# An attention scan fused with a router: matmuls regrouped by array shape, one-hot rows moved to another engine, and table work moved in the order

## The chip, the cores and the metric

The kernel runs on one core of a Trainium2 chip. The metric is device microseconds (us) of one execution. A core has five engines that work side by side, each through its own list of instructions in order: PE (TensorE, matrix products), DVE (VectorE), ACT (ScalarE), POOL (GpSimd) and SP (SyncE, which issues DMA transfers). Engines wait for each other through semaphores.

## The reference

The program chains three layers; the output of one is the input of the next.

```python
def _attn_ref(q, k, v, alpha):            # 4 batches, 8 heads, 768 steps, head size 48
    state = np.zeros((B, H, D, D))
    for t in range(S):
        state = alpha[:, :, t, :, None] * state + np.einsum('bhd,bhe->bhde', k[:, :, t], v[:, :, t])
        y[:, :, t] = np.einsum('bhd,bhde->bhe', q[:, :, t], state)

def _moe_ref(x, w_gate, w_noise, noise, w1, w2):   # 3072 tokens of 384, 8 experts of 1024
    noisy_logits = x @ w_gate + np.log1p(np.exp(x @ w_noise)) * noise
    # the two largest per token; softmax over the two (+ 1e-9 in the denominator)
    for e in range(E):
        for k in range(2):
            mask = top2[:, k] == e
            out[mask] += top2_w[mask, k, None] * (np.maximum(x[mask] @ w1[e], 0.0) @ w2[e])

def _moe2_ref(x, w_gate, w_val, w_out):            # 384 -> 1536 -> 384
    gate = 1.0 / (1.0 + np.exp(-(x @ w_gate)))
    return (gate * (x @ w_val)) @ w_out
```

Inputs are float32, but for the three weights of the last layer, which are float64 and are turned into float32 on the chip.

## The kernel before

**Attention and router.** The scan is done in 6 chunks of 128 steps by 4 pairs of heads: 24 units u = (chunk c, pair p), batches side by side. The order of every engine is written out by hand in this stage. `unit` issues, in turn: the scores of unit u+1 (`st_S`, tile `sc`, L110; copied by ACT to `am` and masked on POOL by an affine_select, L113), the steps of the router's slot TURN, the output (`st_Y`, tile `y`: state part L136, masked part L141), the new state (`st_U`, tile `uu`: the old state through an identity matrix, L154, and keys by values, L159), transposes (`st_K`, L121; `st_R`, L177), the slot COUNT, the scaled copy of the state on ACT, the products of decays three units ahead on DVE (`st_T`, L92 to L98), and the slots DECIDE and LAST. So an instruction that stands late in a unit on PE or DVE keeps the next unit's work behind it.

A chunk's router steps are spread over the units that follow by a table `when`, one pair (unit after the chunk's end, slot) per step: logits (L188), softplus and noise (`router_soft`), choice of two experts (`router_choice`, L331 to L347, with 0/1 rows `mb`), counting by triangular and all-ones matrices (`router_count`, L359 to L362), rank within the expert (`router_rank`, L375 to L395), then the table of rows: for k = 0, 1 a one-hot of the low seven bits of the rank times the token number (`ohl`, eight ACT operations, L410 and L413), a one-hot of the expert and the high bits (`ohh`, DVE, L416), four matmuls into a tile `tb` (L423) and an add into `tab` on DVE (L426). After chunk 3 the table is cast to indices (L449), and the first half of expert 0 is gathered from DRAM by POOL (`early_fetch`, L532).

**Experts.** Each of 8 experts runs in two halves. Float32 operands are split in a high and a low part, and each product takes three matmuls (L507 to L509). Weights come in pieces of 128x768: SP loads `raw`, ACT copies the high part `whi` (L455), and the low part `wlo` is a subtraction (L456) on POOL; for four pieces of expert 0, amid attention, on DVE (`by_vector`). The router steps of the last two chunks run amid expert 0 (list `late`), then `ready` casts the second table and gathers expert 0's second half. Amid the other experts `narrow` turns float64 weights into float32 by three DVE operations (L499 to L501).

**Last layer.** Blocks of 384 tokens: each token's two result rows are gathered by POOL (`grow`, L828), weighted and added on DVE (L831, L832), transposed on PE (`pt`, L840), and run through gate (`pg`, then `sg`), value and output. From expert 0 on, the order is set by a planner that places recorded instructions engine by engine.

## Time and profile before

| | us |
|---|---|
| three runs | 1130.45, 1137.29, 1139.26 |
| median | 1137.29 |
| profiled execution | 1136.44 |
| its span | 1134.7 |
| PE busy | 1090.0 (96%) |
| DVE, ACT, POOL busy | 469.7, 405.2, 312.0 |

The span is the time between the first and the last recorded instruction. A busy time adds up the instructions of an engine, so an engine that works at half the clock is busy for longer. "PEclk" is the clock that was granted to PE in a stretch, 1.00 for 2.4 GHz and 0.50 for 1.2 GHz. Waits are named by the instruction that ended last before the waiting one could start.

### The profile page before, as it was taken

To read this page: it belongs to the slowest core of one execution; us is meant where nothing else is said; L and a number is where in the kernel's file an instruction comes from. 1 tells how busy PE (TensorE), PEld (TensorE's weight loads), DVE (VectorE), ACT (ScalarE), POOL (GpSimd) and SP (SyncE) were. 2 spreads that over 40 slices of the span, in tenths; PEclk is the share of its full clock that TensorE was granted. 3 is DMA by queue.
4 is the path that set the end of the run, shared out by engine and by line. 5 is a ranking of instruction groups with operands and counts; after the bars stand their busy time and mean duration, and the time that the engine had idled before them with its cause. 6 is when DMAs were issued, how large, how long until landed. Compare 5 with 4: busy or idle time off the path is not lost. (4 is left out here: it accounts for less than half of the span.)

```text
span 1134.7 us, 17977 instructions
## 1 busy us (share of the span) xinstructions
PE 1090.0 (96%) x7202; PEld 1039.6 (92%) x7202; DVE 469.7 (41%) x998; ACT 405.2 (36%) x902; POOL 312.0 (27%) x258
## 2 busy tenths in 40 slices
PE   7999988899999999999999989999999999999998
PEld 7777778799898989999999889999999999999998
DVE  8977766325436353534222343052423232313131
ACT  4676657423233333334233425031313131313131
POOL 3332234623333333434331737220101011000000
PEclk8988889999999999999999999999999999999999
DMA  8655523524545454645332531211010101010000
GB/s 230 195 168 169 165 95 112 164 70 143 198 138 188 151 182 157 212 157 184 92 104 56 165 94 49 65 42 43 17 48 14 49 13 51 9 35 1 22 1 21
DMA packets 48072, 115.45 MB, mean 102 GB/s; under 512 B 6464, under 2 KB 24800, under 8 KB 47984
## 3 DMA queue, kind: packets, MB, share of 16 engines
q1 hardware_dynamic: 41456, 94.60, 26.8%
q0 software_dynamic: 6528, 19.67, 5.7%
q8 instruction: 57, 0.93, 0.3%
q14 instruction: 31, 0.25, 0.1%
HBM read 87.50 MB, written 26.74 MB: 101 GB/s over the span
## 5 line engine op out<-in xcount | busy, mean ns | idle before, releaser
L456 POOL TENSOR_TENSOR wlo<-raw,whi 128x768 fp32r<-128x768 f32 x78 | 144.7, 1863 | 250.4 <-ACT whi L455 246.2
L507 PE MATMUL pg<-x2h,whi 128*128 128x384 f32 x576 | 195.2, 339 | 2.6 <-DVE sg L858 2.6
L509 PE MATMUL pg<-x2h,wlo 128*128 128x384 f32 x576 | 193.3, 336 | 0.0
L508 PE MATMUL pg<-x2l,whi 128*128 128x384 f32 x576 | 193.3, 336 | 0.0
L570 DVE SCALAR_TENSOR_TENSOR h<-ph,h 128x384 fp32r<-128x384 f32 x192 | 78.9, 442 | 202.5 <-ACT h L567 195.5
L858 DVE TENSOR_TENSOR sg<-sg,pg 128x384 f32<-128x384 f32 x96 | 53.1, 553 | 213.8 <-PE pg L509 198.8
L507 PE MATMUL ph<-xh,whi 128*128 128x384 f32 (+1 forms) x384 | 136.3, 356 | 2.2 <-DVE h L570 1.6
L508 PE MATMUL ph<-xl,whi 128*128 128x384 f32 (+1 forms) x384 | 136.1, 354 | 0.0
L509 PE MATMUL ph<-xh,wlo 128*128 128x384 f32 (+1 forms) x384 | 135.7, 353 | 0.0
L507 PE MATMUL py<-whi,h 128*128 128x384 f32 x384 | 132.9, 346 | 0.8 <-ACT yrow L593 0.6
L508 PE MATMUL py<-wlo,h 128*128 128x384 f32 x384 | 127.9, 335 | 0.0
L567 ACT ACTIVATE h<-ph 128x448 fp32r<-128x448 f32 (+1 forms) x128 | 65.4, 516 | 174.8 <-PE ph L509 173.3
L509 PE MATMUL py<-whi,h 128*128 128x384 f32 x384 | 118.4, 337 | 3.6 <-DVE h L570 3.6
L828 POOL DMA_INDIRECT grow<-yd,row x48 | 46.9, 977 | 266.7 <-PE pt L840 198.1
L507 PEld LDWEIGHTS pg<-x2h,whi 128*128 128x128 f32 x576 | 108.7, 189 | 3.1 <-DVE sg L858 2.9
L509 PEld LDWEIGHTS pg<-x2h,wlo 128*128 128x128 f32 x576 | 108.7, 189 | 0.0
L508 PEld LDWEIGHTS pg<-x2l,whi 128*128 128x128 f32 x576 | 108.6, 189 | 0.0
L455 ACT ACTIVATE gh<-sg 128x384 fp32r<-128x384 f32 x96 | 50.3, 524 | 140.7 <-DVE sg L858 136.3
L507 PE MATMUL po<-whi,gh 128*128 128x384 f32 x288 | 96.3, 334 | 2.1 <-issue 2.1
L509 PE MATMUL po<-whi,gl 128*128 128x384 f32 x288 | 96.2, 334 | 0.0
L508 PE MATMUL po<-wlo,gh 128*128 128x384 f32 x288 | 96.2, 334 | 0.0
L455 ACT ACTIVATE whi<-raw 128x768 fp32r<-128x768 f32 x82 | 68.6, 842 | 65.2 <-DMA raw<-in_w2h_dram 43.4
(169 smaller groups left out, 1778.2 us busy)
## 6 DMA issues: line engine op xcount, KB each, us to landing
ur<-in_uh_dram SPq DMA_DIRECT2D x23, 675.5 KB
raw<-in_w1h_dram SPq DMA_DIRECT2D x32, 384.0 KB
raw<-in_w2h_dram SPq DMA_DIRECT2D x32, 384.0 KB
yd<-yrow SPq DMA_DIRECT2D x48, 192.0 KB
w<-t SPq DMA_DIRECT2D x36, 192.0 KB
raw<-w SPq DMA_DIRECT2D x18, 384.0 KB
xv<-in_vh_dram SPq DMA_DIRECT2D x6, 768.0 KB
xd<-xr SPq DMA_DIRECT2D x6, 768.0 KB
```

The source lines that it names most:

```text
L455: a = nc.scalar.activation(hi, src, AF.Copy)
L456: b = e.tensor_tensor(lo, src, hi.bitcast(FT), op=OP.subtract)
L507: nc.tensor.matmul(out, wh, mh, start=first, stop=False)
L508: nc.tensor.matmul(out, wh, ml, start=False, stop=False)
L509: nc.tensor.matmul(out, wl, mh, start=False, stop=last)
L567: a = nc.scalar.activation(h[:, :tot], p[:, :tot], AF.Relu)
L570: b = nc.vector.scalar_tensor_tensor(h[:, lo:lo + j - i], p[:, i:j], 0.0, h[:, i:j].bitcast(FT), op0=OP.max, op1=OP.subtract)
L828: nc.gpsimd.indirect_dma_start(out=r, out_offset=None, in_=src, in_offset=bass.IndirectOffsetOnAxis(ap=g.row[:, n, k:k + 1], axis=0))
L858: nc.vector.tensor_tensor(sg, sg, pp[1], op=OP.mult)
```

## The change

Seven things are done:
- The eight score matmuls of a unit, 48 rows by 128 columns of the array, become sixteen of 64x64 tiles (row group j, column half h); the identity product of the state is split in column pieces of 64 and 48. Groups of equal array shape now follow one another.
- A one-hot row is one POOL operation (compare, then multiply) in place of two ACT operations.
- Tables of chunks 0 to 3 are summed in a PSUM bank (`g.ptab`, the tile `wm`), with one copy at the end in place of eight adds.
- Rank keeps counts in a spare column of `mb`; rows and weights of tokens are computed once for all chunks (`router_rows`) in `ready`, amid expert 0.
- In `when` the first table matmul moves from (3, COUNT) to (4, COUNT) and the second to (5, COUNT), with their one-hots and adds; `early_fetch` moves one unit later.
- `by_vector` goes: the four early lower halves of weights are computed on POOL.
- The first operations of `narrow` and of the weighted rows become scalar_tensor_tensor with a broadcast second input; in the last expert weight steps are issued behind the last gather.

```diff
         for b in range(B):
-            for j in range(2):
-                sl = slice(64 * j, 64 * j + D)
-                nc.tensor.matmul(s[j][:, b], KT[u][sl, b, :], Q[u][sl, b, :], start=True, stop=True)
+            for h in range(2):
+                for j in range(2):
+                    sl, hs = slice(64 * j, 64 * j + D), slice(64 * h, 64 * h + 64)
+                    nc.tensor.matmul(s[j][hs, b], KT[u][sl, b, hs], Q[u][sl, b, :], start=True, stop=True)
         for j in range(2):
             nc.scalar.activation(am[:, j], s[j], AF.Copy)
             g.last_mask = nc.gpsimd.affine_select(out=am[:, j], in_=am[:, j], pattern=[[0, B], [1, C]],
...
         if c:
-            nc.tensor.matmul(o[:RW].rearrange("p b e -> p (b e)"), ident[:RW, :RW], st[p][:RW, :B * D], start=True,
-                             stop=False, skip_group_check=True)
+            for j in range(2):
+                hs = slice(64 * j, min(64 * j + 64, RW))
+                nc.tensor.matmul(o[hs].rearrange("p b e -> p (b e)"), ident[:RW, hs], st[p][:RW, :B * D], start=True,
+                                 stop=False, skip_group_check=True)
         for b in range(B):
             for j in range(2):
                 h0 = b * HD + (2 * p + j) * D
...
-    w = t("w", [128, B, 3])
-    nc.vector.tensor_tensor(w[:, :, 0], m8[:, :, 1], m8[:, :, 0], op=OP.subtract)
-    nc.scalar.activation(w[:, :, 1], w[:, :, 0], AF.Exp)
-    v.update(ei=ei, m=m, mb=mb, w=w)
-
-
-def router_count(tc, g, v):
+    nc.vector.tensor_tensor(m, g.iota8.rearrange("p (k b) e -> p k b e", k=2), ei[:, :, :, None].to_broadcast([128, 2, B, E]),
+                            op=OP.is_equal)
+    nc.vector.tensor_tensor(g.mb[c % 2][:, 0:B], m[:, 0], m[:, 1], op=OP.add)
+    v["m"] = m
+
+
+def router_count(tc, g, c, v):
 
     nc = tc.nc
     B, E = g.B, g.E
...
+    g.run = g.mb[(c + 1) % 2][:, B]
+    with nc.allow_low_precision("counts up to 24 are exact"):
+        nc.vector.tensor_reduce(g.run, g.mb[c % 2].rearrange("p b e -> p e b"), axis=mybir.AxisListType.X, op=OP.add)
     if c > g.c0:
         rs = t("rs", [128, B, E])
         nc.vector.tensor_tensor(rs, rk, g.roff[:, None, :].to_broadcast([128, B, E]), op=OP.add)
         rk = rs
-    for k in range(2):
-        nc.vector.tensor_tensor(m[:, k], m[:, k], rk, op=OP.mult)
-    rank = t("rank", [128, 2, B])
-    nc.vector.tensor_reduce(rank.rearrange("p k b -> p (k b)"), m.rearrange("p k b e -> p (k b) e"), axis=mybir.AxisListType.X, op=OP.add)
+    nc.vector.tensor_tensor(m, m, rk[:, None].to_broadcast([128, 2, B, E]), op=OP.mult)
+    nc.vector.tensor_reduce(rank, m, axis=mybir.AxisListType.X, op=OP.add)
     ri = t("ri", [128, 2, B], I32)
     nc.vector.tensor_copy(ri, rank)
     nc.vector.tensor_scalar(ri, ri, 7, None, op0=OP.logical_shift_right)
     nc.vector.scalar_tensor_tensor(kb(g.code[:, T]), ei, float(g.N // 128), ri, op0=OP.mult, op1=OP.add)
     nc.vector.scalar_tensor_tensor(kb(g.low[:, T]), ri, -128.0, rank, op0=OP.mult, op1=OP.add)
-    nc.vector.tensor_scalar(g.nlow[:, T], g.low[:, T], -1.0, None, op0=OP.mult)
-    nc.vector.tensor_scalar(ei, ei, float(g.cap), None, op0=OP.mult)
-    nc.vector.scalar_tensor_tensor(kb(g.row[:, T]), rank, float(g.cap - 1), ei, op0=OP.min, op1=OP.add)
-    nc.vector.tensor_scalar(w[:, :, 2], w[:, :, 1], 1.0, 1e-9, op0=OP.add, op1=OP.add)
-    nc.vector.reciprocal(g.wts[:, T, 0], w[:, :, 2])
-    nc.vector.tensor_tensor(g.wts[:, T, 1], w[:, :, 1], g.wts[:, T, 0], op=OP.mult)
+
+
+def router_rows(tc, g, rw):
+
+    nc = tc.nc
+    t = lambda name, shape: rw.tile(shape, FT, name=name, tag=name, bufs=1)
+    w = t("w", [128, g.NT, 2])
+    nc.vector.tensor_tensor(w[:, :, 0], g.m8[:, :, 1], g.m8[:, :, 0], op=OP.subtract)
+    nc.scalar.activation(w[:, :, 0], w[:, :, 0], AF.Exp)
+    nc.vector.tensor_scalar(w[:, :, 1], w[:, :, 0], 1.0, 1e-9, op0=OP.add, op1=OP.add)
+    nc.vector.reciprocal(g.wts[:, :, 0], w[:, :, 1])
+    nc.vector.tensor_tensor(g.wts[:, :, 1], w[:, :, 0], g.wts[:, :, 0], op=OP.mult)
+    e = t("ec", [128, g.NT, 2])
+    nc.vector.tensor_scalar(e, g.ei, float(g.cap), None, op0=OP.mult)
+    nc.vector.scalar_tensor_tensor(g.row, g.rank, float(g.cap - 1), e, op0=OP.min, op1=OP.add)
 
 
 def router_table(tc, g, c):
...
-            nc.scalar.activation(lo[:, b], g.iotaP, AF.Abs, bias=g.nlow[:, n, k:k + 1])
-        for b in range(B):
-            n = c * B + b
-            nc.scalar.activation(lo[:, b], lo[:, b].bitcast(FT), AF.Relu, bias=g.ids[:, n:n + 1], scale=g.nids[:, n:n + 1])
+            nc.gpsimd.tensor_scalar(lo[:, b], g.iotaP, g.low[:, n, k:k + 1], g.ids[:, n:n + 1], op0=OP.is_equal, op1=OP.mult)
...
-        tab = v["tab"] = g.pst("tb", [128, EN])
+        own = c > g.c0
+        tab = v["tab"] = g.pst("tb", [128, EN]) if own else g.ptab
         for b in range(B):
-            nc.tensor.matmul(tab, lo[:, b], hi[:, b], start=b == 0, stop=b == B - 1)
-
-    def add():
-        nc.vector.tensor_tensor(g.tab, g.tab, v["tab"], op=OP.add)
+            nc.tensor.matmul(tab, lo[:, b], hi[:, b], start=b == 0 and (own or c == k == 0), stop=b == B - 1,
+                             skip_group_check=True)
+
+    def add(k):
+
+        if c > g.c0:
+            nc.vector.tensor_tensor(g.tab, g.tab, v["tab"], op=OP.add)
+        elif c == g.c0 and k == 1:
+            nc.vector.tensor_copy(g.tab, g.ptab)
...
-        nc.vector.tensor_scalar(t, raw[:, :, 1], 3, 0x3FFFFFFF, op0=OP.logical_shift_left, op1=OP.bitwise_and)
+        nc.vector.scalar_tensor_tensor(t, raw[:, :, 1], 3, self.mask.to_broadcast([128, 384]), op0=OP.logical_shift_left,
+                                       op1=OP.bitwise_and)
...
-        with tc.issue_after(a.ins), tc.issue_after(b.ins):
+        with tc.issue_after(a.ins), tc.issue_after(b.ins), behind():
...
-                    nc.gpsimd.indirect_dma_start(out=r, out_offset=None, in_=src,
-                                                 in_offset=bass.IndirectOffsetOnAxis(ap=g.row[:, n, k:k + 1], axis=0))
+                    g.got = nc.gpsimd.indirect_dma_start(out=r, out_offset=None, in_=src, in_offset=bass.IndirectOffsetOnAxis(
+                        ap=g.row[:, n, k:k + 1], axis=0)).ins
                     ga.append(r)
-                nc.vector.tensor_scalar(ga[0], ga[0], g.wts[:, n, 0:1], None, op0=OP.mult)
+                nc.vector.scalar_tensor_tensor(ga[0], ga[0], g.wts[:, n, 0:1], g.zero.to_broadcast([128, g.DM]),
+                                               op0=OP.mult, op1=OP.add)
...
-        when = [(0, COUNT), (1, TURN), (1, DECIDE), (2, COUNT), (2, DECIDE), (5, COUNT), (5, DECIDE), (3, TURN),
-                (3, COUNT), (4, TURN), (4, COUNT), (4, DECIDE)]
+        when = [(0, COUNT), (1, TURN), (1, DECIDE), (2, COUNT), (2, DECIDE), (3, COUNT), (3, DECIDE), (3, TURN),
+                (4, COUNT), (4, DECIDE), (5, COUNT), (5, DECIDE)]
...
-        u0 = g.c0 * NP + NP + 4
+        u0 = g.c0 * NP + NP + 5
         plan_a[u0][DECIDE].append(early_fetch)
         for d in range(3):
...
-        def by_vector(h):
-            g.weights.low = nc.vector
-            h()
-            g.weights.low = nc.gpsimd
-
         for i, (f, h) in enumerate(w0[:4]):
             plan_a[2 + 4 * i][LAST].append(f)
-            plan_a[5 + 4 * i][LAST].append(lambda h=h: by_vector(h))
+            plan_a[5 + 4 * i][LAST].append(h)
         for i, (f, _) in enumerate(w0[4:7]):
             plan_a[20 + i][LAST].append(f)
         start()
@@ -1004,6 +1020,7 @@
 
         def ready():
             idx = nxt["idx"] = router_index(tc, g)
+            router_rows(tc, g, g.rw)
             overflow_plan(tc, g, plan)
             nxt["steps"], nxt["x"] = expert_x(tc, g, 0, *halves[1], g.sx, idx, g.xd)
             nxt["steps"][0]()
```

**The order around a one-hot row (amid attention).** ACT before: `am` is the copy of scores, `xt` of outputs, `st_138` the state, `d_133` the decays' first column.

```order
L169 ACTIVATE st_138<-uu,pd 112x48 x4
L76 ACTIVATE d_133<-ur_129 112x4
L112 ACTIVATE am<-sc 128x512 x2
L410 ACTIVATE ohl<-iotaP,nlow 128x128 x4
L413 ACTIVATE ohl<-ohl,ids,nids 128x128 x4
L144 ACTIVATE xt<-y 128x512
```

POOL with the change, around the first two weight pieces; `ids` are token numbers.

```order
L469 TENSOR_TENSOR wlo<-raw,whi 128x768
L115 AFFINE_SELECT am<-am 128x512 x4
L420 TENSOR_SCALAR ohl<-iotaP,low,ids 128x128 x4
L115 AFFINE_SELECT am<-am 128x512 x2
L420 TENSOR_SCALAR ohl<-iotaP,low,ids 128x128 x4
L115 AFFINE_SELECT am<-am 128x512 x2
L469 TENSOR_TENSOR wlo<-raw,whi 128x768
```

The eight ACT operations are gone from ACT's list, and four operations on POOL stand between the masks of two units; a weight piece's subtraction stands there too.

**POOL from the hand-over to expert 0's second half.** Before, from the masks of the attention stage on:

```order
L113 AFFINE_SELECT am<-am 128x512 x42
L532 DMA xrow<-xd,idx 128x384 x3
L113 AFFINE_SELECT am<-am 128x512 x4
L456 TENSOR_TENSOR wlo<-raw,whi 128x768 x8
L532 DMA xrow<-xd,idx 128x384 x3
L532 DMA xrow<-xd,idx 64x384
L532 DMA xrow<-xd,idx 128x384
L456 TENSOR_TENSOR wlo<-raw,whi 128x768 x3
```

With the change, from the one-hots of the second table of chunk 3 on:

```order
L420 TENSOR_SCALAR ohl<-iotaP,low,ids 128x128 x4
L115 AFFINE_SELECT am<-am 128x512 x2
L546 DMA xrow<-xd,idx 128x384 x3
L115 AFFINE_SELECT am<-am 128x512 x2
L420 TENSOR_SCALAR ohl<-iotaP,low,ids 128x128 x4
L469 TENSOR_TENSOR wlo<-raw,whi 128x768 x3
L420 TENSOR_SCALAR ohl<-iotaP,low,ids 128x128 x4
L469 TENSOR_TENSOR wlo<-raw,whi 128x768 x3
L420 TENSOR_SCALAR ohl<-iotaP,low,ids 128x128 x4
L469 TENSOR_TENSOR wlo<-raw,whi 128x768 x2
L420 TENSOR_SCALAR ohl<-iotaP,low,ids 128x128 x4
L469 TENSOR_TENSOR wlo<-raw,whi 128x768 x3
L546 DMA xrow<-xd,idx 128x384 x3
```

The first three gathers stand before the last unit's two masks, where they stood before the last two units' four; ahead of the second half's gathers stand eleven subtractions, where eight stood, and four groups of one-hots.

**PE around a table matmul, one unit.** Before:

```order
L121 MATMUL tr<-ident,kt 128x112 x4
L177 MATMUL tr<-ident,xt 128x128 x4
L423 MATMUL tb<-ohh,ohl 128x56 x4
L110 MATMUL sc<-qt,kt 128x128 x8
L136 MATMUL y<-qt,st_136 64x128 x8
L141 MATMUL y<-am,xv_131 64x128 x8
L154 MATMUL uu<-st_136,ident 112x192
```

With the change, the unit of the first table of chunk 0:

```order
L181 MATMUL tr<-ident,xt 128x128 x4
L431 MATMUL wm<-ohh,ohl 128x56 x4
L192 MATMUL tr<-xt,wpad 32x128 x16
L112 MATMUL sc<-qt,kt 64x128 x16
L200 MATMUL tr<-ident,ls 128x128
L138 MATMUL y<-qt,st_139 64x128 x8
L143 MATMUL y<-am,xv_133 64x128 x8
L158 MATMUL uu<-st_139,ident 64x192
L158 MATMUL uu<-st_139,ident 48x192
```

The table matmul now stands ahead of the next chunk's logits, one unit later; scores are sixteen matmuls into 64 partitions each, and the identity product two.

## Rows read from the trace of the kernel before

**Rows 1.** Page, section 2: granted clock in tenths, 40 equal slices of the span.

```profile
PEclk8988889999999999999999999999999999999999
```

**Rows 2.** PE's waits: line waited for, total us, times, longest us.

```profile
PE tb L423 <- ACT ohl L413: 11.8, 4, 3.3
...
PE pt L840 <- DVE grow L832: 3.3, 1, 3.3
...
PE pg L507 <- DVE sg L858: 2.6, 1, 2.6
```

**Rows 3.** Table by stretch: us, busy by engine, granted clock, DMA share, GB/s.

```profile
89.00:99.24 10.24, 9.42 (x71) 7.63 (x72) 8.52 (x13) 8.42 (x25) 2.42 (x2) 0.50 0.47 129
...
60.98:91.32 30.34, 27.61 (x343) 22.78 (x343) 23.38 (x59) 20.29 (x64) 9.27 (x8) 0.84 0.52 156
...
211.88:215.29 3.41, 3.41 (x10) 2.60 (x11) 1.78 (x3) 1.71 (x3) 3.25 (x3) 0.50 0.71 196
```

**Rows 4.** Timeline of ACT at 88 us: start, duration, instruction, idle before it.

```profile
88.11 1.28 ACT L410 ACTIVATE ohl<-iotaP,nlow 128x128 fp32r<-128x128 f32 x4 [3.74 <-DVE nlow L390]
```

**Rows 5.** Timeline of PE in one unit at full clock, and the logits.

```profile
69.99 1.08 PE L188 MATMUL tr<-xt,wpad 128*32 128x128 f32 x32
...
76.47 1.16 PE L110 MATMUL sc<-qt,kt 48*128 48x128 f32 x16
...
77.57 1.09 PE L136 MATMUL y<-qt,st 48*64 48x128 f32 x16
...
79.61 0.58 PE L154 MATMUL uu<-st,ident 112*112 112x192 f32 x2
```

**Rows 6.** Groups of DVE, two chunks (60.98 to 121.79 us): busy us, mean ns.

```profile
L456 DVE TENSOR_TENSOR wlo<-raw,whi 128x768 fp32r<-128x768 f32 x2 | 1.9, 958 | 2.0 <-ACT whi L455 2.0
...
L416 DVE TENSOR_TENSOR ohh<-codes,code 128x224 fp32r<-128x224 f32 x4 | 1.5, 385 | 0.0
...
L426 DVE TENSOR_TENSOR tab<-tab,tb 128x56 f32<-128x56 f32 x4 | 0.8, 210 | 5.6 <-PE tb L423 5.6
...
L394 DVE RECIPROCAL wts<-w 128x4 f32<-128x4 f32 x2 | 0.4, 180 | 0.1
...
L346 DVE TENSOR_TENSOR w<-m 128x4 f32<-128x4 f32 x2 | 0.3, 160 | 0.0
```

**Rows 7.** Groups of POOL, whole span: busy us, mean ns, idle before by releaser.

```profile
L456 POOL TENSOR_TENSOR wlo<-raw,whi 128x768 fp32r<-128x768 f32 x78 | 144.7, 1863 | 250.4 <-ACT whi L455 246.2 <-DMA raw<-in_w1h_dram 2.4 <-issue 1.7
...
masks.py:199 POOL TENSOR_SCALAR_AFFINE_SELECT ident<-ident 128x128 f32<-128x128 f32 x1 | 0.3, 291 | 0.0
```

**Rows 8.** Timeline of DVE at the hand-over: index, first and last of the choice.

```profile
160.29 0.19 DVE L449 CAST idx<-tab 128x56 int32<-128x56 f32 x1
...
166.57 0.47 DVE L331 TENSOR_TENSOR nl<-ex,noise 128x32 f32<-128x32 f32 x1
...
169.33 0.19 DVE L344 TENSOR_TENSOR mb<-m 128x32 bf16<-128x32 f32 x1
```

**Rows 9.** Timeline of POOL amid expert 0: first two of five gathers, then subtractions.

```profile
203.56 0.96 POOL L532 DMA_INDIRECT xrow<-xd,idx  x1
...
204.83 0.94 POOL L532 DMA_INDIRECT xrow<-xd,idx  x1 [0.31 <-issue]
...
209.53 5.35 POOL L456 TENSOR_TENSOR wlo<-raw,whi 128x768 fp32r<-128x768 f32 x3
```

**Rows 10.** Timeline of POOL and DVE amid two of the experts.

```profile
343.54 2.08 DVE L501 SCALAR_TENSOR_TENSOR t<-raw,t 128x384 int32<-128x384 int32 x1
...
647.76 5.39 POOL L456 TENSOR_TENSOR wlo<-raw,whi 128x768 fp32r<-128x768 f32 x3
...
647.91 5.47 DVE L831 TENSOR_SCALAR grow<-grow,wts 128x384 f32<-128x384 f32 x1
...
654.55 0.41 DVE L831 TENSOR_SCALAR grow<-grow,wts 128x384 f32<-128x384 f32 x1
```

More of the change, by code (lines that the diff above doesn't have):

```diff
@@ L1 @@
 import math
-from contextlib import ExitStack
+from contextlib import ExitStack, nullcontext
 import concourse.bass as bass
@@ L72, in attention @@
     warm = pst("wm", [128, C])
+    g.ptab = warm[:, :g.E * g.NB]
     def st_D(u):
@@ L211, in count @@
         def count():
-            router_count(tc, g, v)
+            router_count(tc, g, c, v)
         def rank():
@@ L218, in round_steps @@
         return [logits, soft, lambda: router_choice(tc, g, c, v), count, rank, *fix,
-                lambda: hot(0), lambda: mm(0), lambda: (add(), hot(1)), lambda: mm(1), add]
+                lambda: hot(0), lambda: mm(0), lambda: (add(0), hot(1)), lambda: mm(1), lambda: add(1)]
     def fill(k):
@@ L297, in router_consts @@
     g.load_noise = lambda: nc.sync.dma_start(g.noise, g.nh)
-    g.run = c.tile([128, E], BF, name="run")
-    nc.vector.memset(g.run, 0.0)
+    g.mb = [c.tile([128, B + 1, E], BF, name=f"mb{i}") for i in range(2)]
+    nc.vector.memset(g.mb[0][:, B], 0.0)
+    g.zero = c.tile([128, 1], FT, name="zero")
+    nc.vector.memset(g.zero, 0.0)
     g.roff = c.tile([128, E], FT, name="roff")
@@ L305, in router_consts @@
     g.low = c.tile([128, g.NT, 2], FT, name="low")
-    g.nlow = c.tile([128, g.NT, 2], FT, name="nlow")
-    g.nids = c.tile([128, g.NT], FT, name="nids")
-    nc.vector.tensor_scalar(g.nids, g.ids, -1.0, None, op0=OP.mult)
+    g.m8 = c.tile([128, g.NT, 8], FT, name="m8")
+    g.ei = c.tile([128, g.NT, 2], FT, name="ei")
+    g.rank = c.tile([128, g.NT, 2], FT, name="rank")
     g.tab = c.tile([128, E * g.NB], FT, name="tab")
-    nc.vector.memset(g.tab, 0.0)
 def router_soft(tc, g, v):
@@ L332, in router_choice @@
     nc.vector.tensor_tensor(nl, nl, lg, op=OP.add)
-    m8 = t("m8", [128, B, 8])
+    m8 = g.m8[:, T]
     i8 = t("i8", [128, B, 8], U32)
@@ L358, in router_count @@
     rf = rk.rearrange("p b e -> p (b e)")
-    nc.tensor.matmul(rf, g.tri, mf, start=True, stop=False, skip_group_check=True)
+    nc.tensor.matmul(rf, g.tri, mf[:, :B * E], start=True, stop=False, skip_group_check=True)
     for s in range(1, B):
         nc.tensor.matmul(rf[:, s * E:], g.ones, mf[:, :(B - s) * E], start=False, stop=False, skip_group_check=True)
-    nc.tensor.matmul(rf, g.ones, g.run[:, None, :].to_broadcast([128, B, E]), start=False, stop=True,
-                     skip_group_check=True)
+    nc.tensor.matmul(rf, g.ones, mb[:, B:B + 1].to_broadcast([128, B, E]), start=False, stop=True, skip_group_check=True)
 def router_rank(tc, g, c, v):
@@ L372, in router_rank @@
     kb = lambda x: x.rearrange("p b k -> p k b")
-    ei, m, mb, w, rk = (v[x] for x in ("ei", "m", "mb", "w", "rk"))
-    red = t("red", [128, E])
-    nc.vector.tensor_reduce(red, mb.rearrange("p b e -> p e b"), axis=mybir.AxisListType.X, op=OP.add)
-    nc.vector.tensor_tensor(g.run, g.run, red, op=OP.add)
+    m, rk = v["m"], v["rk"]
+    ei, rank = kb(g.ei[:, T]), kb(g.rank[:, T])
+    g.run = g.mb[(c + 1) % 2][:, B]
+    with nc.allow_low_precision("counts up to 24 are exact"):
+        nc.vector.tensor_reduce(g.run, g.mb[c % 2].rearrange("p b e -> p e b"), axis=mybir.AxisListType.X, op=OP.add)
     if c > g.c0:
@@ L558, in expert @@
     hs = []
+    behind = lambda: tc.issue_after(g.got) if g.got is not None else nullcontext()
     for f in range(FB):
@@ L598, in expert @@
         nc.sync.dma_start(g.yd[r0:r0 + n, :], y[:n])
-        with tc.issue_after(b.ins):
+        with tc.issue_after(b.ins), behind():
             bg.step(2)
@@ L620, in narrow_steps @@
     g.w32 = [tc.dram_tile([w.shape[0], 128, 1536], FT, name="w32") for w in g.w32]
+    m = g.weights.mask = g.rc.tile([128, 1], I32, name="mask")
+    tc.nc.vector.memset(m, 0)
+    tc.nc.vector.tensor_scalar(m, m, 0x3FFFFFFF, None, op0=OP.bitwise_or)
     return [lambda w=w, n=n, i=i, s=slice(c, c + 384): g.weights.narrow(w[i][:, s], n[i][:, s])
@@ L929 @@
     g.c0, g.H0 = 3, 384
+    g.got = None
     tile_wise = dict(bufs=1, reuse_waits="tile")
```

7 lines of the change are left out of this document (2 added, 5 removed).

## The prediction

> **What bounds the kernel now.** I read the page's second section first, for the clock by slices, then PE's waits, then tables by stretch and by line, and single rows last. PE is the engine whose time counts: it waits little, so an edit pays where it removes one of its waits, PE work, or a fall of its clock. The clock is below full in the slices up to about 170 us and nearly full after [rows 1]: the fused attention stage is the place to look.
>
> PE's longest wait there is one kind: four times it waits for ACT's one-hot rows, 11.8 us in all [rows 2]. Each of these four stalls lies in a stretch of exactly 10.24 us at 0.50 (the 1.2 GHz level), in which PE is still busy 9.42 us (that of the second) [rows 3]. So a stall costs twice: the wait, and half of the work in the stretch, 4 x 9.42/2 = 18.8 us. Together 30.6 us. The chunk between two such stalls lasts 30.34 us with PE busy 27.61 and DVE 23.38 [rows 3].
>
> Why PE waits: the one-hots stand in the same unit as the rank, and ACT sat 3.74 us until DVE had `nlow` [rows 4]; eight ACT operations later PE may go.
>
> **The change, part by part.** The sum is made against the profiled execution, 1136.44 us (span 1134.7), which is 0.85 under the median of the runs, 1137.29.
>
> *The four stalls.* The first table matmul now stands a unit after its one-hots, so one-hots that are late by 3 us have a unit, some 5 us, to arrive. The most this gives is 30.6 us, unless PE's own need shrinks too. PE's need for a chunk at full clock: 27.61 - 9.42/2 = 22.9 us. To this comes the array shape. A unit runs scores, state part, masked part, identity, update. The two identity passes of 192 columns take 0.58 us; y's 8 pairs of 128 columns take 1.09 [rows 5], 0.136 a pair, so that two passes of 192 need 0.41 at y's rate, and 0.17 is left for the change of shape. I take 0.15 for each of three changes fewer per unit (sc to y, y's masked part to identity, identity to update): 0.45. At most all of the 0.58 is such cost, halved over the changes on its two sides: 0.87 per unit; at least nothing, or a loss of 0.3 if the two identity pieces run one after another. Per chunk of four units 1.8: PE needs 21.1 us.
>
> The sc group itself has twice the matmuls on a quarter of the array each. If four tiles run side by side it stays at 1.16 us. For it: the logits, four column tiles, put 32 passes in 1.08 us, where sc's 16 take 1.16 [rows 5]. But no row shows row and column tiles at once, so two rivals below go by the other ends. The Trainium skill, "TensorE: Matmul & The Clock Gate", Measured speedup vs the span model, has tiles of distinct rows and columns starting about 4 ns apart, and 16 of them 10.6 times as fast as one after another; by that the sum stays as it is and the two rivals drop out; no row here shows such tiles.
>
> DVE's need for a chunk: it loses one lower half of a weight piece (0.96), two table adds (0.42), eight small rank operations of 0.16 to 0.18 (1.34) [rows 6], and two products with m become one (0.13, an estimate from these): 2.85 in all, so 23.38 - 2.85 = 20.5. POOL gains that weight piece (1.86 there) and eight one-hots. Their price is not in the trace; the nearest row is the 128x128 affine_select, 0.29 us, and the other end the 128x768 subtraction with 1.86 [rows 7]. I take 0.35, near the row of the same size, a little up for the second operation. That is 4.7 us of new POOL work, and some of it holds DVE up: a DVE operation that starts under a POOL subtraction takes until that ends (below). Ends 0 and 4.7; I take half, 2.3. DVE needs 22.8 us and, just above PE's 21.1, sets the chunk. Gain 30.34 - 22.8 = 7.5, four times: **-30**. At 1.86 per one-hot POOL would need 9.27 + 1.86 + 14.9 = 26 us a chunk and set it; the gain would be 17.
>
> Against the move to POOL speaks the Trainium skill, "GPSIMD Engine Reference", section 4.1 (Engine selection): elementwise work belongs on VectorE, GPSIMD being about half as fast with two inputs and near equal with one. Rows: the same subtraction took 0.958 on DVE and 1.863 on POOL [rows 6, 7], which agrees. But eight one-hots on DVE, 0.27 each if scaled from the 224-column compare of 0.385 [rows 6], would put 2.2 us a chunk on the engine that I find tightest, and take 2.8 from POOL, half of which blocks DVE (1.4): +0.8 a chunk, or 1115 in place of 1112.
>
> *Fewer shape changes in the other eight units*: these wait for DVE's loads at the start and for the router at the end; of 3.6 us I count **-1**.
>
> *Hand-over from attention.* The index for the first gather was cast at 160.29. It now stands behind the choice of chunk 4's experts, which ran 166.57 to 169.5, 3 us of DVE [rows 8], and the three gathers behind it (1.27 from one to the next, 3.8 in all [rows 9]) stand on POOL ahead of the last unit's mask. Behind that mask wait y, its copy and the logits. PE has about 1.2 us of scores to cover it, so 2.6 show, and a fall of the clock as likely as not (+0.9): **+3.5**; ends 0 (the mask's scores come late themselves) and +8 (choice, gathers and mask in a row).
>
> *Second half of expert 0.* POOL's five gathers started at 203.56, with three subtractions after them [rows 9]. Now three more subtractions (5.4 us by that row) and four one-hots (1.4) come before, so xrow lands 7 us later, and the transposes that wait for it stand where they stood, with less PE work ahead. A 3.41 us stretch at half clock was already there [rows 3]; another costs half of it, 1.7. **+8.7**; ends 0 (POOL idles between pieces) and +12.
>
> *Grow.* L831 (0.41 undisturbed) took 5.47 us beside POOL's three subtractions, which caused PE's 3.3, and a like one the 2.6 of `pg` [rows 2, 10]. In the last expert weight steps now come behind the last gather, and POOL's order becomes one subtraction between gathers: **-5.7** (ends -7, some of `py`'s waits included, and 0). The new form of L831 is no escape by itself: L501, a scalar_tensor_tensor of two inputs, also took 2.08 beside one subtraction [rows 10]. The same goes for L499: **0** (-1 to +1). Rows and weights of the router, done once, take some 1.5 us of DVE amid expert 0 under PE's matmuls; without that cover 1.5.
>
> Sum: -30 - 1 + 3.5 + 8.7 - 5.7 = -24.5; 1136.44 - 24.5 = **1112**. With the ends of the hand-over and expert 0 terms and a DVE delay of 0 to 4.7, about 1104 to 1121.
>
> **Rivals.**
> - *The wait moves.* With the table matmuls late, the next of PE's instructions that needs DVE's router is the count, waiting for `mb`; if DVE lags it stalls 2 us there and the clock still falls. For: DVE sets the chunk in my sum. Against: in that list of waits no count stands near the top. Half of the four falls stay (9.4) and half a microsecond of each wait (2): +11, so 1123.
> - *No price at the hand-over and expert 0.* For: of the 250.4 us that POOL idled before its subtractions, 246.2 were waits for ACT's `whi` [rows 7], so POOL may be as far on as before. Against: at 209.53 three ran back to back [rows 9]. Then +12.2 falls away: 1100.
> - *Four tiles go two at a time.* 8 rounds of 0.12 (y's 1.09 less 0.15, by 8) become 16: +0.95 per unit, 23 in 24 units, of which DVE's lead as the bound (22.8 - 21.1 in each of four chunks) takes 7: +16, so 1128.
> - *Other side: the sc tiles run one after another.* 32 passes of 0.12 take 3.8 us where 8 rounds took 0.95: +2.9 per unit, 69 in 24 units, less the same 7: +62, so 1174. It outweighs the gain from +1.3 us a unit on ((24.5 + 7)/24), which is 19 rounds in place of 8. For: no row has such tiles. Against: the logits' 32 passes.
> - *The change doesn't do it:* the clock falls for another reason than the stall, say the rank's or the turn's small passes. Then the four stalls give 11.8 in place of 30: 1130.
>
> **Numbers.** Forecast 0.50; the wait moves 0.17; no price 0.17; two at a time 0.06; one after another 0.05; clock falls anyway 0.05. Range 1098 to 1128: it holds the forecast with its ends, the first three rivals and 1100's lower edge; left out are the last two and tails, under 2 in 10. The forecast's own range is 1104 to 1121. One per cent, about what a measurement of this kernel can tell from no change, is 1125.9 and 1148.7 from the median. Faster: the forecast but for its upper tail (0.47), 1100 (0.16), three quarters of 1123 (0.13), a third of 1128 (0.02): 0.78. Same: what remains of these and the case of 1130: 0.15. Slower: the serial tiles (0.05) and a masks' wait on a slow POOL (0.02): 0.07.
>
> **What would show it.** No wait of PE for ohl in its list of waits, and no stretch of 10.24 us at 0.50 in a chunk: the stall term. Chunks of about 22.8 us from scores to scores, with DVE nearly full: right; PE nearly full instead: DVE's delay was less. sc at 1.1 to 1.2 us for its 32 passes: the tiles run together; 2 or near 4: the rivals. A one-hot near 0.35 on POOL. PE waiting for xrow about 10 us in all near 210: the expert 0 term; below 3: too dear. L831 near 0.45 and no wait for grow or sg over 1 us. The prediction is wrong if half-clock stretches stay where no stall is, or if one POOL operation takes so long that masks become what PE waits for.

## The result, and the profile after

The changed kernel takes 1126.51 us (median of nine runs, 1121.54 to 1130.71) against 1136.55 before (nine runs): ratio 0.9914, 95% interval 0.9889 to 0.9939. That is 10 us, where 24.5 were forecast; the sign and the range held, the size did not. The profiled execution took 1121.54 us (span 1119.8), the fastest of the nine; a second profile of the same kernel below (1129.32 us) has the same waits.

The spans of the two profiled executions, cut at the starts of the same work on PE:

| from, to | before | after | second profile | moved | forecast |
|---|---|---|---|---|---|
| start to the ninth score group | 50.94 | 50.02 | 51.65 | -0.9 | -1 |
| ninth to 23rd score group | 110.34 | 93.04 | 93.25 | -17.3 | -30 |
| 23rd score group to expert 0 | 17.57 | 22.98 | 22.80 | +5.4 | +3.5 |
| expert 0, first half | 33.01 | 40.29 | 41.42 | +7.3 | +8.7 |
| to the last half expert | 414.06 | 407.89 | 411.82 | -6.2 | 0 |
| from there to the end | 508.83 | 505.62 | 506.68 | -3.2 | -5.7 |

PE's waits after (engine, line waited for, total us, times, longest):

```profile
PE wm L431 <- POOL ohl L420: 10.7, 9, 2.1
PE pt L556 <- DMA xrow<-xd,idx: 8.5, 3, 6.6
...
PE y L143 <- POOL am L115: 3.7, 2, 2.9
PE pg L521 <- DVE sg L878: 2.8, 1, 2.8
...
PE pt L860 <- DVE grow L852: 0.8, 1, 0.8
```

Against [rows 2]: the wait for the one-hots is still there, 10.7 us for 11.8, only that it now names POOL; `pt` for grow fell to 0.8, `pg` stayed. New are the last mask (2.9 of the 3.7) and xrow in expert 0. The clock by slices (page, section 2), to be laid beside [rows 1]:

```profile
PEclk9989879799999999999999999999999999999999
```

POOL's groups over the whole span (busy us, mean ns, idle before), and two groups of one-hots in its timeline, the first beside DVE's scans, the second with DVE idle:

```profile
L420 POOL TENSOR_SCALAR ohl<-iotaP,low,ids 128x128 fp32r<-128x128 f32 x48 | 60.9, 1276 | 9.6 <-DVE low L390 4.9 <-PE tb L431 4.6
...
L115 POOL TENSOR_SCALAR_AFFINE_SELECT am<-am 128x512 f32<-128x512 f32 x48 | 45.7, 976 | 28.3 <-ACT am L114 28.3
```

```profile
56.18 7.46 POOL L420 TENSOR_SCALAR ohl<-iotaP,low,ids 128x128 fp32r<-128x128 f32 x4 [1.86 <-DVE low L390]
```

```profile
156.57 3.13 POOL L420 TENSOR_SCALAR ohl<-iotaP,low,ids 128x128 fp32r<-128x128 f32 x4
```

DVE's timeline at these two places: a scan beside the first group, and the first operation after the second, with DVE's idle time before it:

```profile
57.81 1.23 DVE L95 TENSOR_TENSOR_SCAN gi<-ur,d 112x512 f32<-112x512 f32 x1
161.51 0.56 DVE L469 TENSOR_TENSOR xl<-tr,xh 128x384 fp32r<-128x384 f32 x1 [7.65 <-ACT xh L468]
```

A one-hot took 1.28 us on average, 0.78 alone (3.13/4) and 1.87 beside the scans (7.46/4), where 0.35 had been taken. Stretches of the changed kernel (us, busy by engine, granted clock): one chunk at full clock, then the five at half clock from 60 us to the end of expert 0's first half. The first three follow waits for ohl (at 62, 116 and 141 us), the fourth is at the hand-over, the fifth at the wait for xrow:

```profile
92.42:117.68 25.26, 21.52 (x419) 19.29 (x415) 23.14 (x47) 15.02 (x45) 20.61 (x18) 1.00 0.64 183
63.48:73.72 10.24, 10.03 (x119) 8.33 (x120) 7.87 (x20) 3.23 (x12) 8.80 (x9) 0.50 0.93 271
118.09:124.92 6.83, 6.83 (x81) 5.68 (x71) 5.55 (x19) 2.96 (x12) 6.78 (x7) 0.50 0.98 286
141.98:145.39 3.41, 3.41 (x59) 2.48 (x51) 2.45 (x4) 0.51 (x2) 3.41 (x4) 0.50 0.99 322
155.63:165.87 10.24, 8.68 (x65) 6.32 (x65) 1.67 (x3) 4.92 (x9) 9.43 (x9) 0.50 0.20 60
196.59:210.24 13.65, 6.38 (x19) 4.21 (x20) 4.95 (x21) 2.36 (x4) 9.95 (x9) 0.50 0.60 187
```

A chunk at full clock takes 25.26 us with POOL busy 20.61, where before it was 9.27 [rows 3]. A unit on PE at full clock, for [rows 5]:

```profile
74.91 1.10 PE L112 MATMUL sc<-qt,kt 48*64 48x128 f32 x32
75.84 1.05 PE L138 MATMUL y<-qt,st 48*64 48x128 f32 x16
...
77.75 0.50 PE L158 MATMUL uu<-st,ident 112*64 112x192 f32 x4
...
79.70 1.10 PE L112 MATMUL sc<-qt,kt 48*64 48x128 f32 x32
```

Scores now take 0.93 us to the start of y (1.10 before), the identity product 0.50 (0.58); a unit takes 4.79 and, next, 4.68 us in place of 5.34. The 32 score passes on tiles of a quarter of the array took no longer than the 16 on halves, so four tiles ran at a time.

### The profile page after: what moved, and what is told of

The parts are those of the page before. It is cut to its first block, busy times and chain, and to the rows that moved or that the text cites. A ratio compares the mean times of both kernels' runs of the same rounds, so it can differ in the third digit from the quotient of the medians.

```text
span 1119.8 us, 18728 instructions
## 1 busy us (share of the span) xinstructions
PE 1074.2 (96%) x7618; PEld 1032.1 (92%) x7618; DVE 460.3 (41%) x940; ACT 374.1 (33%) x801; POOL 372.1 (33%) x310
## 5 line engine op out<-in xcount | busy, mean ns | idle before, releaser
L469 POOL TENSOR_TENSOR wlo<-raw,whi 128x768 fp32r<-128x768 f32 x82 | 151.7, 1856 | 244.3 <-ACT whi L468 244.2
```

What stands on the lines that cost most here:

```text
L469: b = e.tensor_tensor(lo, src, hi.bitcast(FT), op=OP.subtract)
```

## The experiments

Each is compared with the kernel before in the same batch of runs; ratios have their 95% interval. "Distance" is the time from the ninth to the 23rd score group in the run's profile: 110.3 us before, 93.0 in the changed kernel. The hand-over is the next row of the table above: 17.6 us before, 23.0 in the changed kernel.

**e1: one-hots back on ACT, in the same slot.** (`low` with scale -1 takes the place of `nlow`.)

```diff
-            nc.gpsimd.tensor_scalar(lo[:, b], g.iotaP, g.low[:, n, k:k + 1], g.ids[:, n:n + 1], op0=OP.is_equal, op1=OP.mult)
+            nc.scalar.activation(lo[:, b], g.iotaP, AF.Abs, bias=g.low[:, n, k:k + 1], scale=-1.0)
...
+            nc.scalar.activation(lo[:, b], lo[:, b].bitcast(FT), AF.Relu, bias=g.ids[:, n:n + 1], scale=g.nids[:, n:n + 1])
```

> The changed kernel with one edit undone: the one-hot rows go back from POOL to eight ACT operations (Abs of low minus iota, then Relu). Theory (the one-hot's price on POOL, 1.28 us on average in place of the 0.35 forecast, is what ate the gain): PE no longer waits for ohl, no half-clock stretch between the ninth and the 23rd score group, which lie about 84 us apart in place of 93.0; POOL reaches expert 0's second gathers earlier by its one-hots, so the wait for xrow there shrinks from 8.5 to 3 us or less; in all about 1112 us against 1126.5. Rival (DVE sets the chunk: POOL's extra subtractions and DVE's router work are the bound, the one-hots only fill POOL's idle time): the distance stays at 91 to 93 us, another wait takes the place of that for ohl, and the time stays within 3 us of 1126.5.

Measured 1122.42, ratio 0.9873 (0.9818 to 0.9928); distance 96.9. Neither theory: the distance is 3.9 us longer than with the one-hots on POOL, and the total is shorter because expert 0's first half takes 33.2 us again, for 40.3. POOL's wait went, and another of the same kind came (PE's waits; ACT's timeline in the first chunk):

```profile
PE y L138 <- ACT xt L146: 13.1, 4, 3.3
```

```profile
57.79 1.28 ACT L422 ACTIVATE ohl<-iotaP,low 128x128 fp32r<-128x128 f32 x4 [3.82 <-DVE low L392]
...
60.51 0.58 ACT L146 ACTIVATE xt<-y 128x512 f32<-128x512 f32 x1
```

ACT stood 3.82 us for `low`, with the copy `xt` behind it in its list; y has one buffer, so PE waited for that copy. The rank on DVE is late, and ACT hands that on.

**e2: one-hots on DVE.**

```diff
-            nc.gpsimd.tensor_scalar(lo[:, b], g.iotaP, ...
+            nc.vector.tensor_scalar(lo[:, b], g.iotaP, ...
```

> The changed kernel with the one-hot rows computed by the same operation on DVE in place of POOL. Theory (price of POOL): about 0.25 us each on DVE, 2 us a chunk; no PE wait for ohl; the ninth to the 23rd score group about 86 to 89 us apart (93.0 with POOL); total about 1115. Rival (DVE sets the chunk already): DVE's 2 us a chunk come on top, distance 95 us or more, total 1128 or more.

Measured 1117.85, ratio 0.9842 (0.9792 to 0.9891); distance 89.8; 0.469 us a one-hot on average, not the 0.25 expected here nor the forecast's 0.27:

```profile
L420 DVE TENSOR_SCALAR ohl<-iotaP,low,ids 128x128 fp32r<-128x128 f32 x48 | 19.6, 469 | 0.2
```

The total fits the first theory, but the wait moved to the count, as a rival of the forecast had it:

```profile
PE tb L362 <- DVE mb L350: 7.8, 4, 2.7
```

**e3: the kernel before with the new table of slots alone.**

```diff
-        when = [..., (5, COUNT), (5, DECIDE), (3, TURN), (3, COUNT), (4, TURN), (4, COUNT), (4, DECIDE)]
+        when = [..., (3, COUNT), (3, DECIDE), (3, TURN), (4, COUNT), (4, DECIDE), (5, COUNT), (5, DECIDE)]
...
-        u0 = g.c0 * NP + NP + 4
+        u0 = g.c0 * NP + NP + 5
```

> The kernel before with nothing changed but the table of slots: each table matmul one unit after its one-hots, first gather one unit later. One-hots stay on ACT, scores stay 128 columns wide. Theory (the stall on the late one-hots brought the half clock with it): the 11.8 us of waits for ohl vanish and with them the four stretches of 10.24 us at 0.50; the ninth to 23rd score group, 110.3 us apart before, come to about 83 to 86 (DVE busy 23.4 per chunk); hand-over +4; total 1110 to 1116. Rival (the clock falls for another reason, say the small passes of rank and turn): four stretches at 0.50 remain, distance about 98 us, total about 1126. Rival (the wait moves to the count's matmuls): a wait of PE for mb of 2 us or more per chunk, total about 1123.

Measured 1138.60, ratio 1.0009 (0.9985 to 1.0032): nothing in the total, and none of the three. The profile has two parts that nearly cancel: the distance falls from 110.3 to 104.1, and the hand-over, with its gathers a unit later, grows from 17.6 to 22.1. The wait for ohl is gone and one for `xt` has its place, 3.2 to 3.8 us in each chunk:

```profile
PE y L136 <- ACT xt L144: 14.9, 5, 3.8
```

```profile
57.83 1.28 ACT L410 ACTIVATE ohl<-iotaP,nlow 128x128 fp32r<-128x128 f32 x4 [3.73 <-DVE nlow L390]
...
60.55 0.58 ACT L144 ACTIVATE xt<-y 128x512 f32<-128x512 f32 x1
```

So the step "one-hots that are late by 3 us have a unit to arrive" was wrong for ACT: PE does not need the one-hots, but it needs what stands behind them.

**e4: the kernel before with the array shapes alone.**

```diff
+            for h in range(2):
+                for j in range(2):
+                    sl, hs = slice(64 * j, 64 * j + D), slice(64 * h, 64 * h + 64)
+                    nc.tensor.matmul(s[j][hs, b], KT[u][sl, b, hs], Q[u][sl, b, :], start=True, stop=True)
```

(and the identity product in two pieces)

> The kernel before with nothing changed but the array shapes: sixteen 64x64 score matmuls and the identity product in two column pieces. Theory (PE's need falls by 0.6 us per unit, but DVE's rank and ACT's one-hots set the end of each chunk): a unit at full clock 4.7 us in place of 5.34; the waits for ohl grow, from 11.8 to 14 or more; the four half-clock stretches stay; total 1130 to 1136. Rival (PE sets the chunk): 24 units times 0.6, total about 1122.

Measured 1130.99, ratio 0.9940 (0.9915 to 0.9966): 6 us, at the low end of what the first theory gave (1130 to 1136). Distance 105.1; the wait grew as it said:

```profile
PE tb L426 <- ACT ohl L416: 15.5, 4, 4.2
```

**r_after: the changed kernel again, beside the next three.**

> The changed kernel once more, beside the next three on the same chip: about 1126 us (1121 to 1131 in its nine runs), and a second profile. Every theory expects the same four costs in it: PE's waits for ohl (10.7 us in the first profile), the mask behind the gathers (2.9), xrow in expert 0 (8.5), and half-clock stretches of some 48 us.

Measured 1127.81, ratio 0.9917 (0.9891 to 0.9944). Waits for ohl 10.8, last mask 2.9, xrow 8.4.

**e5: as e1, with the first one-hot in a unit's last slot.**

```diff
-        when = [..., (3, COUNT), (3, DECIDE), (3, TURN),
+        when = [..., (3, COUNT), (3, DECIDE), (3, LAST),
```

> As e1 (one-hots on ACT in the changed kernel), with the first one-hot of a chunk moved from the first slot of a unit to its last, so that on ACT it stands behind the copies xt and km and the state of that unit; its table matmul stays where it is. Theory (what is late is DVE's rank, and whichever engine holds the one-hots ahead of other work for PE hands that lateness on): ACT no longer waits for low with xt behind it, so PE's four waits of 3.3 us for xt go, with their 3.41 us stretches at half clock; the ninth to 23rd score group come from 96.9 us apart to 78 to 84; total about 1108 to 1112. Rival (DVE is the bound, so the lateness shows elsewhere, as in the version with the one-hots on DVE, where the count waited 2 us or more for mb): new waits of PE for mb or qt of 2 us and more each chunk, distance 88 or more, total 1117 or more.

Measured 1109.43, ratio 0.9767 (0.9744 to 0.9790); distance 82.3. Two chunks (stretch, busy by engine, granted clock):

```profile
56.93:80.40 23.47, 21.65 (x415) 19.09 (x415) 22.40 (x47) 19.87 (x62) 9.69 (x9) 1.00 0.70 204
80.40:103.86 23.46, 21.66 (x415) 19.09 (x415) 22.39 (x47) 19.88 (x62) 9.67 (x9) 1.00 0.70 205
```

Full clock, PE 21.65 and DVE 22.40 of 23.47 us. The forecast had 21.1 and 22.8: a chunk near its 22.8 us is here, in a kernel that places the one-hots otherwise. Expert 0's first half takes 33.3 us again.

**e6: the old forms of the first operations of narrow and of the weighted rows.**

```diff
-        nc.vector.scalar_tensor_tensor(t, raw[:, :, 1], 3, self.mask.to_broadcast([128, 384]), ...
+        nc.vector.tensor_scalar(t, raw[:, :, 1], 3, 0x3FFFFFFF, op0=OP.logical_shift_left, op1=OP.bitwise_and)
...
-                nc.vector.scalar_tensor_tensor(ga[0], ga[0], g.wts[:, n, 0:1], g.zero.to_broadcast([128, g.DM]), ...
+                nc.vector.tensor_scalar(ga[0], ga[0], g.wts[:, n, 0:1], None, op0=OP.mult)
```

> The changed kernel with the first operations of narrow and of the weighted rows as tensor_scalar again. My forecast priced both forms alike. If that was right: within 1 us of the changed kernel from the fourth half expert (ph03) to the end. Rival (the new form keeps DVE out of POOL's way): from ph03 to the last layer's second block some 6 to 9 us more than the changed kernel, waits of PE for h and grow of 2 us or more again, total about 1133.

Measured 1128.55, ratio 0.9932 (0.9906 to 0.9958): no difference from r_after that can be told, as forecast. In the changed kernel the new form took 3.59 us beside two POOL subtractions, in e6 the old form 3.41 at the same place (DVE's and POOL's timelines of the changed kernel):

```profile
662.15 3.59 DVE L850 SCALAR_TENSOR_TENSOR grow<-grow,wts,zero 128x384 f32<-128x384 f32 x1 [0.56 <-DMA grow<-yd,row]
```

```profile
662.55 1.01 POOL L469 TENSOR_TENSOR gl<-sg,gh 128x384 fp32r<-128x384 f32 x1
663.52 1.80 POOL L469 TENSOR_TENSOR wlo<-raw,whi 128x768 fp32r<-128x768 f32 x1
```

**e8: the first index ahead of the choice.**

```diff
-        plan_a[u0][DECIDE].append(early_fetch)
+        plan_a[u0][DECIDE].insert(1, early_fetch)
```

> The changed kernel with the index of the first gather cast straight after the table's copy, ahead of the choice of chunk 4's experts on DVE; nothing else moves. Theory (the gathers stand ahead of the last unit's mask on POOL and start late because the cast waits for the choice): gathers start about 2.6 us sooner, PE's wait for the last mask (2.9 us) falls below 1 and with it the 10.24 us at half clock, 23rd score group to the first expert matmul 16 to 18 us in place of 23.0; total about 6 us less than the changed kernel. Rival (the clock falls there for the small transposes that follow): the wait goes but the half-clock stretch stays, gain 2 to 3 us.

Measured 1126.90, ratio 0.9916 (0.9889 to 0.9944): nothing that can be told from r_after; the theory's 6 us did not come. The wait for the mask went; the hand-over took 21.8 us for 22.8. Its end is a chain of ACT's copies and DVE's subtractions, where PE waits in turn (PE's timeline):

```profile
153.51 1.33 PE L138 MATMUL y<-qt,st 48*64 48x128 f32 x16 [0.67 <-ACT xt L146]
...
159.28 0.55 PE L556 MATMUL tr<-ident,xrow 128*128 128x128 f32 x3 [1.18 <-ACT xr L182]
160.26 0.55 PE L556 MATMUL tr<-ident,xrow 128*128 128x128 f32 x3 [0.43 <-DVE xl L469]
161.37 1.12 PE L181 MATMUL tr<-ident,xt 128*128 128x128 f32 x4 [0.56 <-DVE xl L469]
```

**e10: e5 with the old array shapes** (the diff of e4, reversed).

> The version with the one-hots on ACT in a unit's last slot (e5, 1109.4 us), with the old array shapes (eight score matmuls of 128 columns, one identity product). Theory (with the stalls gone DVE, 22.4 us of a chunk of 23.5, hides most of what the shapes cost PE): PE's need rises from 21.6 to about 24 us a chunk (0.6 per unit) and becomes the bound: chunk 24 to 24.5, total 3 to 6 us more than e5, 1112 to 1115. Rival (PE is the bound already): the whole 0.6 times 24 units, 14 us, total 1123.

Measured 1110.59, ratio 0.9776 (0.9748 to 0.9805): not to be told from e5 (1109.43); the rival's 14 us did not come. The theory's chunk of 24 us did, with PE at 23.26 of 24.04:

```profile
56.15:80.19 24.04, 23.26 (x343) 19.36 (x342) 22.97 (x47) 19.75 (x62) 9.41 (x9) 1.00 0.69 198
```

**e11: the kernel before with the table of slots of e5** (e3, and LAST for the first one-hot).

> The kernel before with nothing changed but the table of slots, as in e3 (which left the time where it was), and in it the first one-hot in a unit's last slot. Theory (on ACT the one-hots waited for DVE's rank with the copy xt behind them, wherever the table matmul stood): PE's waits of 3.2 to 3.8 us for xt go, no half-clock stretch between the ninth and the 23rd score group, which lie 84 to 90 us apart (104.1 in e3, 110.3 before); total 1112 to 1118. Rival (DVE, 23.4 us busy in a chunk and with the rank still longer, hands the lateness to the count): waits for mb or qt of 2 us a chunk, distance over 95, total 1125 or more.

Measured 1134.39, ratio 0.9987 (0.9965 to 1.0009): the rival's total. The distance is 99.1, over 95 as the rival had it, and the hand-over takes 24.3 us, so that part of what the stretch gained is given back. The wait is not for mb or qt: ACT no longer holds PE up, and DVE is too late with the other one-hot; half clock follows in every chunk:

```profile
PE tb L423 <- DVE ohh L416: 9.6, 4, 3.5
```

**e12: e5 with the edit of e8.**

> e5 with the index of the first gather cast ahead of the choice (the edit of e8, which took the wait for the mask away and gave 1 us). Theory (the hand-over is a chain through ACT and DVE, and the waits move along it): wait for the mask gone, the 13.65 us at half clock shorter, total 1 to 3 us less than e5, 1107. Rival (the mask was the whole price in e5, where it stood 3.07 us with 13.65 us at half clock): 6 us less, 1103.

Measured 1108.75, ratio 0.9763 (0.9735 to 0.9791): not to be told from e5. The wait for the mask fell from 3.1 to 0.5 us, so the rival, which had put 6 us on it, fell.

**e13: e5 with the early lower halves of weights on DVE** (`by_vector` restored).

> e5 with the four early lower halves of weights back on DVE. Theory (DVE is the bound of a chunk now): 0.96 us more of DVE a chunk and somewhat less blocking by POOL; chunk 23.5 to 24.5 in place of 23.47, total 0 to 4 us more than e5. Rival (POOL's 1.86 blocks DVE for longer than the 0.96 saved): chunk shorter, total 1 to 3 us less.

Measured 1107.27, ratio 0.9776 (0.9741 to 0.9811): not to be told from e5. A chunk takes 23.14 us in its profile:

```profile
54.57:77.71 23.14, 21.49 (x414) 19.12 (x415) 22.07 (x48) 19.67 (x62) 9.15 (x8) 1.00 0.72 207
```

DVE is busy for 22.07 us, where e5 has 22.40, although the subtraction (0.96 [rows 6]) is back in its list. By these rows the subtraction on POOL lengthened DVE's other operations by some 1.3 us a chunk, about what DVE saved (an estimate).

**e14: e5 with eight more small operations per chunk on DVE.**

```diff
+    if c <= g.c0:
+        for _ in range(8):
+            nc.vector.tensor_scalar(kb(g.wts[:, T]), rank, float(g.cap), None, op0=OP.mult)
```

> e5 (one-hots on ACT in a unit's last slot) with eight small operations more per chunk on DVE, behind low in the rank, some 1.4 us, whose results nobody reads: about what the change took out of the router on DVE. Theory (e11, the kernel before with the same slots, was 25 us slower than e5 because its DVE has that work, and DVE sets the chunk): chunk 24.8 us or more in place of 23.5, waits of PE for ohh or mb, total at least 5 us more than e5, and up to 20 more if these waits bring the half clock back. Rival (DVE's small operations fit in its idle time; what e11 lacked is something else): within 2 us of e5.

Measured 1119.04, ratio 0.9840 (0.9812 to 0.9868): as the theory had it, 9.6 us more than e5 by the medians and 8 by the ratios, for 1.4 us a chunk, and half clock in three stretches again before the hand-over. PE waits:

```profile
PE wm L439 <- DVE ohh L431: 8.4, 4, 2.9
```

**e15: e5, e12 and e13 together.**

> e5 with the early weight halves on DVE (e13) and the index cast ahead of the choice (e12): 1105 to 1109 us, if these two give 0 to 2 us each as they did alone.

Measured 1109.92, ratio 0.9770 (0.9743 to 0.9797): no better than e5.

**e16: e5 with unread one-hots on POOL as well.**

```diff
+                x = g.aw.tile([128, 128], FR, name="spare", tag="spare", bufs=1)
+                nc.gpsimd.tensor_scalar(x, g.iotaP, g.low[:, n, k:k + 1], g.ids[:, n:n + 1], op0=OP.is_equal, op1=OP.mult)
```

> e5 with the one-hots of chunks 0 to 3 computed on POOL too, into a tile that nobody reads: POOL is as busy in the attention stage as in the changed kernel, but PE waits for ACT's. Theory (the changed kernel lost by waiting for the one-hots themselves, 1.28 us each): masks come later by a few tenths, total 0 to 4 us more than e5, so 1109 to 1113. Rival (a busy POOL costs by itself, by masks that come late behind one-hots and by DVE operations that it holds up): half or more of the 17 us between e5 and the changed kernel, 1118 or more.

Measured 1114.87 (1109.04 to 1123.22), ratio 0.9810 (0.9772 to 0.9847): between the theory and the rival. A chunk takes 24.4 to 24.8 us, at full clock, with POOL busy for 21.08 of the 24.41 shown and DVE for 23.34; PE's waits for masks come to 8.9 us:

```profile
80.51:104.92 24.41, 22.21 (x416) 19.40 (x415) 23.34 (x47) 19.77 (x62) 21.08 (x17) 1.00 0.66 197
```

```profile
PE y L143 <- POOL am L115: 8.9, 13, 2.2
```

From e5 to the changed kernel the distance grows by 10.7 us and expert 0's first half by 7.0. A busy POOL alone brings the distance to 85.8, so it makes 3.5 of the 10.7. For the rest the changed kernel's trace has PE's waits for the one-hots and the clock that falls with them; but there the first one-hot of a chunk also stands in a unit's first slot, here in its last. POOL's one-hots in the last slot were not run, so engine and slot are not parted.

## Why the prediction was wrong, step by step

**The step that failed: the four stalls, -30 forecast, -17.3 measured.** Its mis-sized term is the one-hot on POOL: "I take 0.35, near the row of the same size", measured 0.78 alone and 1.28 on average. With it the cover failed: the late one-hots had been given a unit, some 5 us, to arrive, and a group of four took up to 7.46 us by itself. So PE waits nine times for the one-hots, 10.7 us for 11.8, and the clock falls with some of these waits: 10.24, 6.83 and 3.41 us at 0.50, where four stretches of 10.24 had been. The affine_select of the same size [rows 7] was no measure for a compare and a multiply by per-partition numbers. That the other end of the term (1.86 a one-hot) gave a gain of 17 is luck: there POOL needs 26 us and sets the chunk, while in the chunk of 25.26 us POOL was busy for 20.61, and e16 has POOL as busy in chunks of 24.4 to 24.8.

Behind the wrong size lies a wrong picture of the lateness. The forecast gave late one-hots a unit to arrive. e3 shows that on ACT this takes 6 us off the distance and not 30, since `xt` is queued behind them; e1 shows the same wait; e11 shows that with ACT out of the way DVE's own half, `ohh`, is late. e5 has three things together, and none of e1, e3, e11 has all: one-hots behind ACT's copies, DVE's router cut down, the table matmul a unit later (which goes with the first: a one-hot in a unit's last slot comes behind that unit's COUNT slot). That the cut on DVE counts is shown by e14 and not only by elimination: 1.4 us put back in each of four chunks cost 8 to 10 in all. The price on POOL does not decide alone: in the same slot one-hots on ACT (e1) left the distance 3.9 us longer than those on POOL. Whether 0.35 us a one-hot on POOL would have given the forecast's chunk is open.

**The rest of the sum.** PE's need of a chunk (21.1) was near, by e5 (21.65). That DVE's 22.8 is near e5's 22.40 is in part luck: half of the 2.8 us of one-hots on POOL was counted in it as blocking, and e5 has none there; e16, which has them, is at 23.34. The shape term was near: 0.55 to 0.66 us per unit for 0.45, but where DVE is nearly full it gives less: 0.57 us a chunk of four units between e10 and e5, and nothing that can be told in the total.

Expert 0's second half cost 7.3 for 8.7, with the parts wrong. The forecast counted four one-hots ahead of the gathers (1.4 us); the order has four groups of four, and they took 3.1 to 3.5 us each, 13 in all. POOL's timeline, up to the first gather:

```profile
189.44 3.25 POOL L420 TENSOR_SCALAR ohl<-iotaP,low,ids 128x128 fp32r<-128x128 f32 x4
192.67 5.34 POOL L469 TENSOR_TENSOR wlo<-raw,whi 128x768 fp32r<-128x768 f32 x3
198.17 1.05 POOL L546 DMA_INDIRECT xrow<-xd,idx  x1 [0.16 <-DVE ofr L657]
```

This gather started 32.1 us after expert 0's first matmul, 24.7 before and 25.4 in e5, where the one-hots are on ACT, eight subtractions stand ahead as before, and the stretch costs 0.3. The last group of one-hots ended at 26.7 us by that count (22.0 on ACT in e5), and the index needs it; three more subtractions, which e5 has behind the gathers, stand between that and the first gather. No run here has one-hots on POOL in this stretch without the three subtractions, so that their shares are not parted.

The hand-over cost 5.4 for 3.5; that it hangs on the mask alone was wrong (e8). Grow: -3.2 for -5.7; PE's 3.3 fell to 0.8, and not by the form (0.4 in e6); that the order of the weight steps did it is the forecast's reading, which no run tried alone. `pg` kept its 2.8 by the mechanism named: the DVE operation ahead of `sg` (662.15, shown with e6) ended 0.4 us after POOL's subtraction. The -6.2 amid the experts was not forecast; it is -2.2 in the second profile, so that most of it differs from one execution to the next. What sets it was not tried.

**The rivals.** "The wait moves to the count" is what e2 did; in the changed kernel the first chunk alone shows it (1.4 us). "No price at the hand-over and expert 0" fell: 5.4 and 7.3 us were paid. Both rivals on serial score tiles fell: 1.10 us for 32 passes. The Trainium skill, "TensorE: Matmul & The Clock Gate", Measured speedup vs the span model, where tiles of distinct rows and columns overlap, agrees with that row. "The clock falls for another reason" fell: in e5 the rank's and turn's passes are all there and the clock is 1.00 in the chunks.

The Trainium skill's "GPSIMD Engine Reference", section 4.1 (Engine selection), which spoke against the move, was right in its advice (e2 is some 8 us faster than the changed kernel by the two ratios); that with one input POOL is near DVE's rate did not hold here, 0.469 us on DVE against 0.78 at best on POOL. The forecast weighed it as +3 against the DVE version and had the sign of that wrong; its 0.27 a one-hot on DVE (0.22 by width alone) was low too.

## What to carry to other kernels

Before a late result is given more time, look at what stands behind its producer in that engine's list: the wait passes to whoever needs that. The price of an operation that the trace does not show is not read from one of equal size and another kind; if the ends of the range decide the sum, the far end is the forecast as much as the near one. Where the clock hangs on waits, a small delay costs more than its length: 1.4 us of DVE work in each of four chunks, 5.6 in all, cost 8 to 10 us (e14). So count what else is near to being late. And a total that does not move can hide two changes that nearly cancel (e3): cut the span at the same work in both kernels.
